# K by DMA transpose, its four taps as diagonal products on TensorE, a full complex product, and one planned order for all engines

## The chip, the cores and the metric

The kernel runs on one core of one Trainium2 chip. A core has a matrix engine (TensorE, PE in the profile, with PEld for its weight loads), a vector engine (VectorE, DVE), an activation engine (ScalarE, ACT), GpSimd (POOL) and SyncE (SP), which here issues every DMA. All share an on-chip memory of 128 partitions; TensorE writes to PSUM, from which VectorE or ScalarE must copy.

The metric is the device time of one execution in microseconds. The kernel before took 290.25 us (median of three runs, 289.12 to 290.41).

## The reference

x is A_q, 2048 rows (time) by 640 columns. Two branches are computed from it and mixed by a gate.

```python
def _A_ref(q, k, v, shift_k, ssm_k, ssm_D):
    k_shift = sum over t of k_pad[:, t:t + S, :] * shift_k[:, ks - 1 - t]     # four taps along time
    kv = k_shift * v
    y = irfft(rfft(kv, 2 * S) * rfft(ssm_k, 2 * S))[:S]                        # a causal convolution, per column
    y = y + kv * ssm_D
    return q * y

def _B_ref(x, w1, w2, w3, w4):
    h = gelu(layernorm(x) @ w1)
    hs = (four groups of h's columns, moved by +1, -1, +2, -2 rows) @ w2
    x1 = x + hs
    return x1 + gelu(layernorm(x1) @ w3) @ w4

g = sigmoid((x * gate_w).sum(-1, keepdims=True))
return g * _A_ref(x, ...) + (1 - g) * _B_ref(x, ...)
```

(The first two lines are shortened: the reference pads, transforms over the padded length 4096 and cuts.) All inputs and the output are bf16; w1 and w2 are 640x640, w3 640x1536, w4 1536x640.

## The kernel before

Time is split as t = 16 p + t1: partition p holds 16 rows, and a "row group" t1 is one row of each partition, 128x640. Branch B works on 128x512 and 128x128 matmuls: `mlp1` (w1, in 4 chunks of 4 row groups, ScalarE applies gelu), `w2` (16 row groups, VectorE adds x and sums), `w3` (4 chunks of 6 pairs) and `w4` (16 row groups). x and x1 are normalized by `x_stats`, `x_transpose` and `x1_norm` and transposed by DMA from SBUF.

Branch A's transform of length 4096 is done as four passes of small matmuls, with a trip through DRAM between them. `step1` multiplies the 64 time points of each row group with the table F1, for the filter h (8 calls on HT) and for kv (8 calls on KV), and writes to S_h and S_x. `gather` reads these in another order. `step2` multiplies with T2 (32 frequency groups for h and 32 for x, four to a call); the result holds real parts in partitions 0 to 63 and imaginary parts in 64 to 127. `product` multiplies h and x. `step3` multiplies with the inverse tables and writes to S_g, `gin` reads S_g, and `step4` multiplies with F4, with q and the gate, and adds to x1.

In F1 the two halves of the partitions hold even and odd 16-row blocks, so that step1 is two matmuls of 64 rows each, in two halves of the array.

The parts that the change touches:

- **Taps.** `kv_load` brings K in with three rows of halo (18 DMAs on SP), `kv_consts` spreads the tap factors over the partitions, and `kv_compute` works on VectorE alone: per pair of row groups four products with the factors (line 458), three sums (463), one product with v (464).
- **Product.** `product` (lines 365 to 367) makes the two cross products (64 partitions each) and the straight products, three VectorE operations per call. It leaves the real and imaginary sums to step3, which multiplies the straight products with I1 and the cross products with I2 into one PSUM tile (378, 380).
- **Tables.** `table` (289) spreads the sines in CMP to T2, I1 and I2 on GpSimd. They lie in the buffer (tag RT) that HT leaves free after step1.
- **Order.** The string ORDER names the steps. For SP the first 139 names are issued in exactly this order; all other instructions are placed by the framework's scheduler, on each engine, when the program is built. A letter in a step's name says which engine copies from PSUM (A is ScalarE, V VectorE, G GpSimd).

PSUM holds two tiles for branch A (`psc`) and two for branch B (`psm`).

## Time and profile before

| | before |
|---|---|
| median of three runs | 290.25 us |
| the profiled execution | 289.77 us, its span 288.0 us |
| busy: TensorE, VectorE, ScalarE, GpSimd | 237.0, 233.1, 161.8, 67.2 us |
| mean granted TensorE clock | 0.957 |
| DMA | 58.77 MB, mean 204 GB/s |
| VectorE on the taps (lines 458, 463, 464) | 59.9 us |
| table loads of ScalarE | ten, 1283 ns each |

Busy time of TensorE is the union of its matmuls, each from start to modelled end; matmuls overlap, so a busy TensorE is not one at its peak, and its work is better read from start to start. The groups of instructions give, behind the shape and the count, the busy time of the group, the mean of one in ns, and the idle time of the engine just before, with what ended it.

### The profile page before, as it was taken

How to read it: one execution, taken by the hardware profiler on the slowest of the kernel's cores; microseconds unless marked ns; L12 is line 12 of the kernel's file. 1: busy time of each engine (PE TensorE's matmuls, PEld its weight loads, DVE VectorE, ACT ScalarE, POOL GpSimd, SP SyncE). 2: the span in 40 equal slices, each digit the busy share in tenths (PEclk: the TensorE clock that was granted, in tenths of full speed). 3: DMA queues.
4: the chain of work that ended last, by engine and by line, in shares of the span. 5: the costliest groups of instructions: out<-in, count | busy, mean ns of one | idle time of the engine just before them, and what ended most of it. 6: DMA issues, size and time to landing. Idle time of an engine off the chain costs nothing.

```text
span 288.0 us, 4142 instructions
## 1 busy us (share of the span) xinstructions
PE 237.0 (82%) x1486; PEld 114.6 (40%) x1486; DVE 233.1 (81%) x438; ACT 161.8 (56%) x234; POOL 67.2 (23%) x57
## 2 busy tenths in 40 slices
PE   0167499599999799996199999999999999998670
PEld 0023134367554232433034555544455544454330
DVE  3888999979999999779851888689899969622894
ACT  4949896486848699563055425365234566600651
POOL 3122223002878030059871000000010000000442
PEclk9999889879999999999579999999999999999997
DMA  7496894471999589592369964483786660298283
GB/s 263 156 216 124 184 238 93 169 229 36 342 235 260 175 278 378 220 347 107 63 223 321 230 222 138 162 287 98 246 285 210 201 218 23 109 278 333 97 257 114
DMA packets 51692, 58.77 MB, mean 204 GB/s; under 512 B 25427, under 2 KB 42580, under 8 KB 51160
## 3 DMA queue, kind: packets, MB, share of 16 engines
q1 hardware_dynamic: 51672, 58.52, 66.2%
q8 instruction: 11, 0.18, 0.3%
q14 instruction: 9, 0.07, 0.1%
HBM read 34.91 MB, written 18.36 MB: 185 GB/s over the span
## 4 chain that ended last, share of the span: by engine, by line
DVE 45%; PE 29%; DMA 9%; issue 6%; POOL 3%; SPq 3%; ACT 2%; POOLq 0%; DVEq 0%; ACTq 0%
PE ps L639 8%; PE ps L658 6%; DVE tmp L458 5%; DMA q<-in_A_q_dram 4%; PE psw L595 4%; PE ps L354 4%; DVE p L366 4%; DVE hs L367 4%; DVE acc L463 3%; DVE p L365 3%; PE pst L313 2%; PE ps L378 2%; DMA WA<-in_B_w_dram 2%; PE ps L329 2%; DVE xn L471 2%
## 5 line engine op out<-in xcount | busy, mean ns | idle before, releaser
L639 PE MATMUL ps<-x1t,W 128*128 128x512 bf16 x240 | 63.2, 386 | 0.0
L658 PE MATMUL ps<-W,gt 128*128 128x512 bf16 (+1 forms) x384 | 60.7, 300 | 0.0
L331 ACT CAST stg<-ps 128x1024 bf16<-128x1024 f32 (+1 forms) x37 | 31.5, 900 | 22.8 <-PE ps L329 16.9
L658 PEld LDWEIGHTS <-gt 128*128 128x128 bf16 x384 | 28.7, 98 | 23.4 <-issue 2.6
L669 POOL TENSOR_SCALAR q<-q,GS 128x640 bf16<-128x640 bf16 x8 | 8.9, 1121 | 121.6 <-DMA q<-in_A_q_dram 63.3
L530 PE MATMUL psm<-xt,WA 128*128 128x512 bf16 x100 | 25.8, 422 | 10.2 <-DMA xt<-xn 8.6
L640 ACT ACTIVATE gt<-ps 128x1024 bf16<-128x1024 f32 x24 | 24.7, 1033 | 13.0 <-PE ps L639 12.9
L639 PEld LDWEIGHTS <-W 128*128 128x128 bf16 x240 | 21.1, 98 | 24.3 <-issue 3.4
L354 PE MATMUL ps<-ax,TB 128*128 128x512 bf16 (+1 forms) x128 | 26.9, 298 | 0.9 <-DVE gs L384 0.4
L659 DVE SCALAR_TENSOR_TENSOR X<-ps,OMG,X 128x640 bf16<-128x640 f32 x16 | 14.1, 880 | 14.8 <-PE ps L658 14.8
L463 DVE TENSOR_TENSOR acc<-acc,tmp 128x1280 bf16<-128x1280 bf16 x24 | 22.9, 955 | 0.4
L595 PE MATMUL psw<-WA,HT 128*128 128x512 bf16 (+1 forms) x116 | 22.8, 312 | 0.6 <-DVE X L599 0.6
L483 POOL TENSOR_TENSOR rs<-ve,EXPO 128x4 f32<-128x4 f32 x8 | 10.6, 1330 | 53.8 <-DVE ve L613 25.1
L458 DVE TENSOR_TENSOR tmp<-K,cj 128x1280 bf16<-128x1280 bf16 (+1 forms) x25 | 22.9, 921 | 0.2
L530 PEld LDWEIGHTS <-WA 128*128 128x128 bf16 x100 | 10.5, 106 | 29.3 <-issue 20.3
L680 ACT CAST y<-ps 128x640 bf16<-128x640 f32 x15 | 10.1, 693 | 20.0 <-PE ps L676 14.9
L358 DVE CAST hs<-ps 128x640 bf16<-128x640 f32 x15 | 11.9, 817 | 9.8 <-PE ps L354 9.8
L356 ACT CAST hs<-ps 128x640 bf16<-128x640 f32 x17 | 11.7, 694 | 14.0 <-PE ps L354 14.0
L289 POOL TENSOR_SCALAR TB<-CMP,sm 128x2048 bf16<-128x2048 bf16 (+1 forms) x8 | 14.6, 1840 | 19.4 <-ACT stg L331 19.4
L356 ACT CAST xs<-ps 128x640 bf16<-128x640 f32 x15 | 10.2, 692 | 14.4 <-PE ps L354 11.9
L354 PEld LDWEIGHTS <-TB 128*128 128x128 bf16 x128 | 12.1, 97 | 15.2 <-issue 5.3
L382 ACT CAST gs<-ps 128x640 bf16<-128x640 f32 x17 | 11.3, 694 | 12.1 <-PE ps L380 11.8
(130 smaller groups left out, 413.5 us busy)
## 6 DMA issues: line engine op xcount, KB each, us to landing
S_h<-stg SPq DMA_DIRECT2D x8, 640.0 KB, 4.2
...
```

The source lines that it names most:

```text
L289: G.tensor_scalar(out=dst, in0=src, scalar1=col(c), scalar2=0.0, op0=ALU.mult, op1=ALU.add)
L331: A.copy(out=stg[:, :, o:o + w], in_=ps[:, :, 0:w])
L354: PE.matmul(ps[:, o:o + w], lhsT=st["T2"][:, g, :], rhs=ax[:, i, o:o + w], start=True, stop=True)
L356: A.copy(out=dst[:, i, :], in_=ps[:])
L458: V.tensor_tensor(out=dst[:, i:i + n, :], in0=K[:, r:r + n, :], in1=cj[:, j:j + 1, :].to_broadcast([P, n, D]), op=ALU.mult)
L463: V.tensor_tensor(out=acc[:], in0=acc[:], in1=tmp[:], op=ALU.add)
L530: PE.matmul(ps[:, v, :].rearrange("p (a b) -> p a b", a=4), lhsT=W1N[:, k, 160 * f:160 * f + P] if f < 4 else W1M[:, k, :], rhs=xt[:, :, k ...
L595: PE.matmul(ps[:, o:o + w], lhsT=h_tile(f, t1), rhs=W2P[:, f, o:o + w], start=(f == 0), stop=(f == 4))
L639: PE.matmul(ps[:, u, :].rearrange("p (a b) -> p a b", a=4), lhsT=st["W3"][:, k, f * P:(f + 1) * P], rhs=xt[:, :, k, :], start=(k == 0), st ...
L640: A.activation(out=gt[:, 2 * (fp % 2):2 * (fp % 2) + 2, :], in_=ps[:], func=ACT.Gelu_apprx_tanh)
L658: PE.matmul(ps[:, o:o + w], lhsT=st["gt", c, f // 4][:, f % 4, i * P:(i + 1) * P], rhs=st["W4"][:, f, o:o + w], start=(f == 0), stop=(f == ...
L659: V.scalar_tensor_tensor(out=X1[:, t1, :], in0=ps[:], scalar=OMG[:, t1:t1 + 1], in1=X1[:, t1, :], op0=ALU.mult, op1=ALU.add)
```

## The change

- **K.** `k_load` transposes K by DMA, straight from DRAM, in four pieces of four row groups, so that columns lie on partitions and KT holds, per row group and block of 128 columns, a 128x128 matrix. `k_wrap` makes the three row groups that reach back over a partition's edge.
- **Taps.** `kv_consts` builds 20 diagonal matrices (5 column blocks by 4 taps) on VectorE. `tap` (16 row groups) makes, per column block, four matmuls of 128x128x128 with KT as weights and a diagonal matrix as moving operand, added in PSUM: transposing back and weighing at once. Then VectorE multiplies with v, from PSUM (V) or behind a copy by ScalarE (A).
- **Rows.** v, the filter and KV now all use t = 16 p + t1. `h_transpose` makes whole 128x128 transposes in place of two halves. F1 is kept twice, with the partitions of one parity set to zero, and step1's two matmuls use all 128 rows.
- **Product.** Two more VectorE operations of 64 partitions form real and imaginary part; step3 has one table I and one matmul pair per group.
- **Tables.** T2 and I are spread by VectorE (letters VV), four operations of 2048 elements.
- **Scaling.** `scale_x1` and `gate_q` may also use ScalarE.
- **End.** `gin` reads in three pieces (8, 6 and 2 row groups) in place of two, and the stores are steps of their own.
- **Order.** Each step is a generator that yields between its instructions on different engines, and a name in ORDER advances its step by one piece. All five engines are issued in exactly the order of the string; the scheduler places nothing. The string is new.

The diff, cut to its core:

```diff
-    k_flat = A_k.rearrange("b s d -> (b s) d")
+    v_rows = A_v.rearrange("b (p t1) d -> (b p) t1 d", t1=NT)
+    k_rows = A_k.rearrange("b (p t1) d -> (b p) (t1 d)", t1=NT)
...
+    def scaled(ev, dst, src, a):
+        if ev == "A":
+            A.activation(out=dst, in_=src, func=ACT.Copy, scale=a)
+        else:
+            (G if ev == "G" else V).tensor_scalar(out=dst, in0=src, scalar1=a, scalar2=0.0, op0=ALU.mult, op1=ALU.add)
...
+    def piped(pairs):
+        last = None
+        for first, second in pairs:
+            first()
+            yield
+            if last is not None:
+                last()
+                yield
+            last = second
+        last()
...
     def step1(name, c, ev):
-                PE.matmul(ps[:, r, 0:w], lhsT=F1[H * r:H * r + H, :], rhs=src[H * r:H * r + H, 2 * c * D + o:2 * c * D + o + w], start=True, stop=True)
+                    PE.matmul(ps[:, r, 0:w], lhsT=F1[:, r, :], rhs=src[:, 2 * c * D + o:2 * c * D + o + w], start=True, stop=True)
...
     def product(s):
         V.tensor_tensor(out=p2[64:128], in0=x[64:128], in1=h[0:64], op=ALU.mult)
+        yield
         V.tensor_tensor(out=h[:], in0=x[:], in1=h[:], op=ALU.mult)
-        st["p", s] = (h, p2)
+        yield
+        V.tensor_tensor(out=h[0:64], in0=h[0:64], in1=h[64:128], op=ALU.subtract)
+        yield
+        V.tensor_tensor(out=h[64:128], in0=p2[0:64], in1=p2[64:128], op=ALU.add)
+        st["p", s] = h
...
     def step3(s, ev):
-                PE.matmul(ps[:, o:o + w], lhsT=st["I1"][:, g, :], rhs=p1[:, i, o:o + w], start=True, stop=False)
-            for (o, w) in pieces(D):
-                PE.matmul(ps[:, o:o + w], lhsT=st["I2"][:, g, :], rhs=p2[:, i, o:o + w], start=False, stop=True)
+                    PE.matmul(ps[:, o:o + w], lhsT=st["I"][:, g, :], rhs=p1[:, i, o:o + w], start=True, stop=True)
...
+    GIN = ((0, 8), (8, 6), (14, 2))
...
-    def kv_compute(c):
...
+    def kv_consts():
+        st["DG"] = pool("A2").tile([P, DC * 4, P], BF16, name="DG")
+        V.tensor_tensor(out=st["DG"][:], in0=IDB[:].unsqueeze(1).to_broadcast([P, DC * 4, P]),
+                        in1=st["cr"][:].rearrange("p k j -> p (k j)").unsqueeze(2).to_broadcast([P, DC * 4, P]), op=ALU.mult)
+
+    def k_load(c):
+        SP.dma_start_transpose(out=st["KT"][:, 4 * c:4 * c + 4].rearrange("p a b c -> p (a b) c"), in_=k_rows[:, 4 * c * D:4 * c * D + 4 * D])
+
+    def k_wrap(ev):
+        st["KW"] = pool("A2").tile([P, 3, DC, P], BF16, name="KW")
+        turn(G if ev == "G" else V, st["KW"][:].rearrange("p a b c -> p (a b) c"), st["KT"][:, NT - 3:NT].rearrange("p a b c -> p (a b) c"), 1)
+
+    def v_load(c):
+        SP.dma_start(out=st["KV"][:, 4 * c * D:4 * c * D + 4 * D].rearrange("p (t d) -> p t d", d=D), in_=v_rows[:, 4 * c:4 * c + 4, :])
+
+    def tap(t1, ev):
+        ps = psc.tile([P, D], F32, name="psk", tag="c")
+        for k in range(DC):
+            for j in range(4):
+                u = t1 - j
+                PE.matmul(ps[:, k * P:k * P + P], lhsT=st["KT"][:, u, k, :] if u >= 0 else st["KW"][:, u + 3, k, :], rhs=st["DG"][:, 4 * k + j, :],
+                          start=(j == 0), stop=(j == 3))
+        yield
+        kv = st["KV"][:, t1 * D:t1 * D + D]
+        if ev == "A":
+            y = ring.tile([P, D], BF16, name="yk", tag="gq", bufs=3)
+            A.copy(out=y[:], in_=ps[:])
+            yield
+            V.tensor_tensor(out=kv, in0=y[:], in1=kv, op=ALU.mult)
+        else:
+            V.tensor_tensor(out=kv, in0=ps[:], in1=kv, op=ALU.mult)
...
+        "open.L1.left open.A2.right kv_alloc consts0 load_cj load_x.2 consts0 k_load.1 t2_table kv_consts "
+        "x_stats.2.AAAA x_stats.2.AAAA k_load.2 t2_table x_stats.2.AAAA x_stats.2.AAAA x_stats.2.AAAA f1_table t2_table "
...
     def emit(names):
         for n in names:
-            f, *args = n.split(".")
-            calls[f](*(int(a) if a.isdigit() else a for a in args))
+            if n not in steps:
+                f, *args = n.split(".")
+                steps[n] = calls[f](*(int(a) if a.isdigit() else a for a in args))
+            if steps[n] is not None:
+                next(steps[n], None)
-    with tc.manual_schedule(engines={mybir.EngineType.SP}):
-        emit(ORDER[:FIRST])
-    emit(ORDER[FIRST:])
+    with tc.manual_schedule(engines={getattr(mybir.EngineType, n) for n in ("PE", "DVE", "Activation", "Pool", "SP")}):
+        emit(ORDER)
```

Three places show what the order now is. The first is SP's queue at the start of the program (X is x, WA holds w1, cr the tap factors, KV first holds v). Before:

```order
L153 DMA X<-in_A_q_dram 128x2560
L156 DMA WA<-in_B_w_dram 128x5x640
L401 DMA cr<-in_A_shift_k_dram 1x2560
L153 DMA X<-in_A_q_dram 128x2560 x2
L479 DMA_TRANSPOSE xt<-xn 128x20x128
L153 DMA X<-in_A_q_dram 128x2560
L479 DMA_TRANSPOSE xt<-xn 128x20x128
L479 DMA_TRANSPOSE xt_268<-xn 128x20x128 x2
```

Now:

```order
L464 DMA cr<-in_A_shift_k_dram 128x5x4
L153 DMA X<-in_A_q_dram 128x2560
L478 DMA_TRANSPOSE KT<-in_A_k_dram 128x20x128 x2
L486 DMA KV<-in_A_v_dram 128x2560 x2
L478 DMA_TRANSPOSE KT<-in_A_k_dram 128x20x128 x2
L486 DMA KV<-in_A_v_dram 128x2560 x2
L153 DMA X<-in_A_q_dram 128x2560
L156 DMA WA<-in_B_w_dram 128x5x640
L370 DMA S_x<-stg 256x1x1280
L153 DMA X<-in_A_q_dram 128x2560
```

K and v come first, behind one chunk of x; w1 and the rest of x come behind them, and the third chunk of x behind step1's first write.

The second place is VectorE at a product (p and hs are products, ps a PSUM tile, X<-ps the sum of w4). Before:

```order
L365 TENSOR_TENSOR p_1853<-xs,hs 64x2560
L358 CAST hs<-ps_1839 128x640
L366 TENSOR_TENSOR p_1853<-xs,hs 64x2560
L659 SCALAR_TENSOR_TENSOR X<-ps_1857,OMG,X 128x640
L367 TENSOR_TENSOR hs<-xs,hs 128x2560
```

Now:

```order
L411 TENSOR_TENSOR p_2033<-xs,hs 64x2560
L413 TENSOR_TENSOR p_2033<-xs,hs 64x2560
L415 TENSOR_TENSOR hs<-xs,hs 128x2560
L717 SCALAR_TENSOR_TENSOR X<-ps_2025,OMG,X 128x640
L417 TENSOR_TENSOR hs<-hs 64x2560
L419 TENSOR_TENSOR hs<-p_2033 64x2560
```

There are five operations in place of three between the copies.

The third place is TensorE in step3, one frequency group. Before:

```order
L378 LDWEIGHTS TB
L378 MATMUL ps_1775<-hs,TB 128x512
L378 LDWEIGHTS TB
L378 MATMUL ps_1775<-hs,TB 128x128
L380 LDWEIGHTS TB
L380 MATMUL ps_1775<-p_1635,TB 128x512
L380 LDWEIGHTS TB
L380 MATMUL ps_1775<-p_1635,TB 128x128
```

Now, with w4 (L714) behind a pair of groups:

```order
L431 LDWEIGHTS TB
L431 MATMUL ps_2035<-hs,TB 128x512
L431 LDWEIGHTS TB
L431 MATMUL ps_2035<-hs,TB 128x128
L431 LDWEIGHTS TB
L431 MATMUL ps_2040<-hs,TB 128x512
L431 LDWEIGHTS TB
L431 MATMUL ps_2040<-hs,TB 128x128
L714 LDWEIGHTS gt
L714 MATMUL ps_2025<-W_1474,gt 128x512
```

Each group has half the matmuls.

More of the change, by code (lines that the diff above doesn't have):

```diff
@@ L278, in i_tables @@
             n = tab([P, NG, 32], "n")
[L279 to L292 removed]
+            ts(n[:], m[:], col(20 + c), op0=ALU.add)
@@ new lines, in i_tables, with table @@
+            yield from sin_table(CMP[:, 1, :, c, :], n, 8192)
+            yield
[4 more added lines that the diff above has]
+            (G if ev == "G" else V).tensor_scalar(out=dst, in0=src, scalar1=a, scalar2=0.0, op0=ALU.mult, op1=ALU.add)
+    def table(which, ev):
+        if "I" not in st:
+            TB = main.tile([P, 2, NG, P], BF16, name="TB", tag="RT")
+            st["T2"], st["I"] = TB[:, 0], TB[:, 1]
@@ L304, in h_transpose, with pair, first, second @@
     def h_transpose(dc):
-        if dc == 0:
+        if "HT0" not in st:
             st["HT0"] = main.tile([P, NT * D], BF16, name="HT0", tag="RT")
-        hv = st.pop(("HN", dc)).rearrange("p (t2 r t1) -> p t1 r t2", t1=NT, r=2)
+        hv = st.pop(("HN", dc)).rearrange("p (t t1) -> p t1 t", t1=NT)
         dst = st["HT0"][:].rearrange("p (t d) -> p t d", t=NT)
-        for hh in range(2):
+        def pair(hh):
             ps = psc.tile([P, 8, P], BF16, name="pst", tag="c")
-            for i in range(8):
-                for r in range(2):
-                    PE.transpose(out=ps[H * r:H * r + H, i, :], in_=hv[:, 8 * hh + i, r], identity=IDB[:])
-            f = A.copy
-            f(out=dst[:, 8 * hh:8 * hh + 8, dc * P:(dc + 1) * P], in_=ps[:])
+            def first():
+                for i in range(8):
+                    PE.transpose(out=ps[:, i, :], in_=hv[:, 8 * hh + i, :], identity=IDB[:])
+            def second():
+                A.copy(out=dst[:, 8 * hh:8 * hh + 8, dc * P:(dc + 1) * P], in_=ps[:])
+            return first, second
@@ L317, in d_fold @@
+        yield from piped(pair(hh) for hh in range(2))
     def d_fold():
@@ L345, in step2, with pair, first, second @@
         ax = st.pop((name, s))
[L346 to L350 removed]
+        dst = []
+        def pair(i):
             g = 4 * s + i
             ps = psc.tile([P, D], F32, name="ps2", tag="c")
[L353 to L359 removed]
+            def first():
+                for (o, w) in pieces(D):
+                    PE.matmul(ps[:, o:o + w], lhsT=st["T2"][:, g, :], rhs=ax[:, i, o:o + w], start=True, stop=True)
+            def second():
+                if not dst:
+                    if name == "h":
+                        dst.append(pool("L2").tile([P, 4, D], BF16, name="hs", tag="hp", bufs=4))
+                    else:
+                        dst.append(pool("C").tile([P, 4, D], BF16, name="xs", tag="xs", bufs=2))
+                    st[name + "s", s] = dst[0]
+                if ev[i] == "A":
+                    A.copy(out=dst[0][:, i, :], in_=ps[:])
+                else:
+                    V.tensor_copy(out=dst[0][:, i, :], in_=ps[:])
+            return first, second
+        yield from piped(pair(i) for i in range(4))
     def product(s):
@@ L388, in gin @@
+        yield from piped(pair(i) for i in range(4))
+        for u in range(2):
+            yield
+            g = 4 * s + 2 * u
+            SP.dma_start(out=bass.AP(tensor=S_g[:].tensor, offset=S_g[:].offset + g * P * D, ap=[[D, P], [P * D, 2], [1, D]]), in_=st["gs", s, u][:])
+    GIN = ((0, 8), (8, 6), (14, 2))
     def gin(q, a):
+        t, n = GIN[q]
         if ("gin", q) not in st:
-            st["gin", q] = (R1("gin0") if q == 0 else pool("L3").tile([P, NT * D], BF16, name="gin1"))[:].rearrange("p (r d) -> p r d", r=2)
@@ L403, in kv_consts @@
[L403 to L417 removed]
+        st["cr"] = ring.tile([P, DC, 4], BF16, name="cr", tag="cr", bufs=1)
```

269 lines of the change are left out of this document (119 added, 150 removed), and 125 rows, old and new, of the table ORDER.

## The prediction

> **What bounds the kernel now.** I read the page first (busy shares and the chain that ended last), then busy time by stretch, then the chain in order of time.
>
> ```profile
> span 288.0 us, 4142 instructions
> PE 237.0 (82%) x1486; PEld 114.6 (40%) x1486; DVE 233.1 (81%) x438; ACT 161.8 (56%) x234; POOL 67.2 (23%) x57
> DVE 45%; PE 29%; DMA 9%; issue 6%; POOL 3%; SPq 3%; ACT 2%; POOLq 0%; DVEq 0%; ACTq 0%
> ```
>
> VectorE and TensorE are equally busy, and the chain runs over VectorE first, over TensorE second. The stretches show that this is not one limit but three, one after another:
>
> ```profile
> 0.00:17.00 17.00, 1.86 (x4) 0.59 (x5) 10.81 (x64) 11.70 (x27) 4.53 (x11) 1.00 0.71 209
> 17.00:36.00 19.00, 13.60 (x49) 5.39 (x49) 17.48 (x65) 15.11 (x21) 4.45 (x4) 0.96 0.78 171
> 36.00:140.00 104.00, 91.58 (x644) 44.05 (x643) 96.31 (x176) 71.72 (x102) 40.44 (x29) 0.94 0.70 215
> 140.00:160.00 20.00, 17.00 (x78) 6.86 (x78) 9.53 (x16) 9.83 (x11) 8.95 (x6) 0.82 0.78 232
> 160.00:252.00 92.00, 90.33 (x559) 45.61 (x558) 78.32 (x84) 42.94 (x59) 0.79 (x1) 1.00 0.58 187
> 252.00:288.00 36.00, 22.63 (x156) 12.12 (x153) 20.70 (x37) 10.52 (x16) 8.08 (x7) 0.94 0.63 216
> ```
>
> The columns are span, then busy time of TensorE, its weight loads, VectorE, ScalarE, GpSimd, then granted clock, DMA share and GB/s. Until 140 us VectorE is the limit (96.31 of 104 in the third stretch). TensorE is busy there too by the record, but it waits between short matmuls. From 160 to 252 TensorE is full (90.33 of 92). The last 36 us belong to waits:
>
> ```profile
> 127.66 2.37 DVE tmp L458
> ...
> 252.46 4.91 DMA S_g<-gs
> ...
> 259.07 7.73 DMA q<-in_A_q_dram
> ...
> 272.73 4.69 DMA q<-in_A_q_dram
> ...
> 284.58 0.49 DVE X L684
> ```
>
> In the tail the chain goes through the last write of S_g and two loads of q. The first row is of another kind: a tap product of 2.37 us, in the stretch in which GpSimd builds the tables.
>
> **The change, part by part.** VectorE first, with the rows that carry its prices:
>
> ```profile
> L458 DVE TENSOR_TENSOR tmp<-K,cj 128x1280 bf16<-128x1280 bf16 (+1 forms) x25 | 22.9, 921 | 0.2
> L463 DVE TENSOR_TENSOR acc<-acc,tmp 128x1280 bf16<-128x1280 bf16 x24 | 22.9, 955 | 0.4
> L458 DVE TENSOR_TENSOR acc<-K,cj 128x1280 bf16<-128x1280 bf16 (+1 forms) x9 | 7.5, 844 | 0.0
> L464 DVE TENSOR_TENSOR KV<-acc,KV 128x1280 bf16<-128x1280 bf16 x8 | 6.6, 827 | 0.1
> L367 DVE TENSOR_TENSOR hs<-xs,hs 128x2560 bf16<-128x2560 bf16 x8 | 11.9, 1489 | 0.2
> L365 DVE TENSOR_TENSOR p<-xs,hs 64x2560 bf16<-64x2560 bf16 x8 | 11.9, 1487 | 0.9 <-ACT hs L356 0.5
> L366 DVE TENSOR_TENSOR p<-xs,hs 64x2560 bf16<-64x2560 bf16 x8 | 11.9, 1484 | 0.1
> L358 DVE CAST xs<-ps 128x640 bf16<-128x640 f32 x17 | 13.7, 821 | 5.3 <-PE ps L354 5.1
> L681 DVE TENSOR_TENSOR y<-y,q 128x640 bf16<-128x640 bf16 x15 | 8.0, 551 | 0.7 <-POOL q L669 0.7
> L669 DVE TENSOR_SCALAR q<-q,GS 128x640 bf16<-128x640 bf16 x8 | 2.9, 382 | 2.1 <-DMA q<-in_A_q_dram 2.1
> L659 DVE SCALAR_TENSOR_TENSOR X<-ps,OMG,X 128x640 bf16<-128x640 f32 x16 | 14.1, 880 | 14.8 <-PE ps L658 14.8
> ```
>
> *Taps leave VectorE:* 22.9 + 22.9 + 7.5 + 6.6 = 59.9 us, all before 142 us, where VectorE sets the pace. *What comes for them:* of the 16 row groups ten go through ScalarE and one multiply (10 x 551 ns = 5.5), six are multiplied from PSUM (6 x 0.82 = 4.9). The 20 diagonal matrices are one product of 2560 elements: between L367's 1.49, whose operands lie side by side, and 2.9 (twice that, since one operand is a repeated element); I take 2.7. *The full product:* two more 64-partition operations per group, 8 x 2 x 1.49 = +23.8. *Copies:* by the order 23 of step2's 64 stay with VectorE (32 before) and 5 of step3's 32 (15 before): 19 x 0.82 = -15.6. *Tables:* the four operations of 2048 elements come from GpSimd: 0.38 (L669, 640 elements) to 1.22 (3.2 times that); I take 1.0, +4. They wait for step1's last read of HT, whose buffer the tables take; TensorE has w4's first groups beside them. Net about -35.
>
> ScalarE takes the copies, and loses table loads (ten before; the order has three):
>
> ```profile
> L331 ACT CAST stg<-ps 128x1024 bf16<-128x1024 f32 x26 | 25.7, 1026 | 21.6 <-PE ps L329 15.7 <-issue 4.6 <-DMA S_x<-stg 0.7
> L601 ACT ACTIVATE jk<-X 128x640 bf16<-128x640 bf16 x16 | 11.9, 743 | 5.2 <-DVE X L599 4.3 <-DVE ve L613 0.9
> L356 ACT CAST xs<-ps 128x640 bf16<-128x640 f32 x15 | 10.2, 692 | 14.4 <-PE ps L354 11.9 <-issue 2.5
> L208 ACT ACT_TABLE_LOAD x4 | 5.1, 1283 | 0.1
> ```
>
> (19 + 10 - 3) x 0.69 = +18, eleven scalings near L601's 0.74 = +8, seven loads less = -9. That is work beside other work, as long as ScalarE is not the longest engine of its stage.
>
> TensorE, by rows that give start to start:
>
> ```profile
> 60.25 1.99 PE L313 MATMUL pst<-IDB,E 128*64 128x128 bf16 x32
> ...
> 85.87 0.22 PE L595 MATMUL psw<-WA,HM 128*128 128x128 bf16 x1
> 86.05 4.48 PE L639 MATMUL ps<-x1t,W 128*128 128x512 bf16 x20
> 90.45 0.61 PE L329 MATMUL ps<-HT,F 64*128 64x512 bf16 x4
> 90.99 1.04 PE L595 MATMUL psw<-WA,HT 128*128 128x512 bf16 x4
> ...
> 208.68 0.61 PE L658 MATMUL ps<-W,gt 128*128 128x128 bf16 x8
> ```
>
> Twenty 512-wide matmuls take 4.48, and the next row starts 4.40 behind them: 220 ns each with the change of form at the end, and I use 216. One 128-wide matmul is on record for 0.22 from start to end, eight of them, each with its own weights, for 0.61: (0.61 - 0.22)/7 = 56 ns from start to start. *Taps:* 16 x 20 x 56 = +17.9. *step3:* one matrix in place of two, 32 x (216 + 56) = -8.7. *step1:* L329's two pairs, side by side, take 0.54 (90.45 to 90.99); with zeros in half the rows the four go one after another, 0.86; over 16 groups, the 256-wide piece included, about +6 (0 to 8.7). *h_transpose:* 160 halves at 62 ns become 80 whole ones at 56 to 125: 0 to -5.5, I take -4. Net +11, in the stages where TensorE idled.
>
> *DMA:* four transposes replace 18 issues of K:
>
> ```profile
> L479 SPq DMA_TRANSPOSE xt<-xn x4: 3019/3069/3158, 12.1 to 27.4; - x4
> ```
> ```profile
> xt<-xn SPq DMA_TRANSPOSE x4, 5.0
> ```
> ```profile
> 3.00:9.00 6.00, 1.86 (x4) 0.49 (x4) 4.00 (x30) 4.05 (x9) 0.11 (x1) 1.00 1.03 402
> 20.00:22.00 2.00, 2.00 (x9) 0.86 (x8) 1.72 (x7) 2.00 (x7) 0.27 (x1) 1.00 1.12 216
> ```
>
> The three rows are x's transposes by issue (least, median, most ns), their landing, and two stretches, the first with plain loads alone, the second with a transpose alone. A transpose of K's size holds SP's queue 3.07 us, lands 5.0 us after issue and moves 216 GB/s where plain loads move 402. These read SBUF; K's will read DRAM, which no row shows: from 3.07 us up, and I take 3.07. Then the two that the first taps need land near 10 us, and all four near 17; VectorE and ScalarE have the tables and a chunk's statistics until then. Behind them on SP stand v, X's chunk 0 and w1. Behind step1's first write to S_x, which waits for its last copy, stand X's chunks 1 and 3: a late chunk of KV delays the statistics too.
>
> **The sum, by stage of the new order.** I counted each engine's instructions between places in the order and priced them by these rows. (1) Up to mlp1's first matmul: TensorE 21, ScalarE 38 (18 passes of statistics, ten copies of taps, six of step1, sines, two table loads), VectorE 37 (the 10.81 + 17.48 of the first 36 us of before hold the same tables and statistics; less 8.7 for the copies of cj and for statistics and normalization that now come later, plus 17 for the taps, their matrices, three copies and F4's table). Before, ScalarE stood idle 9.2 of its first 36 us; with that, 47. (2) mlp1 until w2 starts: TensorE 29.2 (100 x 216 and the rest of step1 and taps), the others 16 to 24. (3) w2 and the filter's step1: TensorE 48.2, ScalarE 47.9. (4) step2 to step3: TensorE 96.3; VectorE 59.6 for products, 22 for copies, 10.6 (12 x 0.88) for w4 and 6 for shorter ones, 98 (the tables' 4 stand beside stage 3's end). (5) step4 and the last of w4: TensorE 28.2, and 4 for the last sum and store; q's last load stands on SP behind two stores that wait for step4's first sums, with some 15 us of TensorE's work ahead of its use. Stages 2 to 5 run at the share that the busiest engine reaches: 96.31/104 = 0.93 or 90.33/92 = 0.98; I take 0.955. So 47 + 30.6 + 50.5 + 102.7 + 29.5 + 4 = 264.3 us of span. Span to time is 289.77 - 288.0 = 1.8: **266 us** (the profiled run lies 0.5 below the median of 290.25, which is less than the rounding here). Against before: stages 1 to 3 end at 128, where TensorE's full stretch begins at 160 now (-32), stage 4 takes 103 where that stretch took 92 (+11), and the tail is 33.5 where it was 36 (-2.5).
>
> **Rivals.**
>
> *A. The order works nearly without waits.* Stages 2 to 5 at 0.98, stage 1 at 44 us: 44 + 29.8 + 49.2 + 100 + 28.8 + 4 = 256, time 258. For it: 160:252 shows 0.98 already, and GpSimd, beside which a tap took 2.37 us, loses the tables. Against: stage 3 has two engines within 1%, stage 4 two within 2%; in 160:252 VectorE had only 78 of 92.
>
> *B. VectorE bounds stage 4.* Each group now waits for 7.4 us of products (4.5 before) between step2 and step3. If neither engine hides the other and the busier reaches 0.85: 98/0.85 = 115, 12.6 more, 279 us. Against: w3 and w4, 70 us of TensorE's 96, do not depend on the products.
>
> *C. Slower: K's transposes from DRAM.* All of stage 1 hangs on them: no tap, no KV, and behind them on SP no X and no w1. At 216 GB/s they run at half of the 402 of plain loads. If their small pieces go at a third of that out of DRAM, each holds the path 9 us instead of 3, stage 1 grows by 4 x 6 = 24 and the time is 290; it is slower than before from about 9.5 us each. The Trainium skill ("DMA: Bandwidth & Descriptors", Specifications) puts line rate at transfers of 512 B and up, which speaks for this; how far below it DRAM lies, no row shows.
>
> *D. A cold TensorE in stage 1.*
>
> ```profile
> PEclk9999889879999999999579999999999999999997
> ```
>
> Each digit is a fortieth of the span, 7.2 us. The 5 stands at 137 to 144 us, right behind a stretch without matmuls: there TensorE had half its clock. In stage 1 it has 21 us of work in 47. At half clock the 320 taps cost 112 ns each, 36 us instead of 18, and with step1's the stage 42 us of TensorE beside 38 and 37 of the others. Three equal engines at 0.85 make 49, with six of the ten us ahead of the first tap 55: 8 more, 274 us. Against it: the first 36 us of before show 0.96 to 1.00 with TensorE idle for more than half. The Trainium skill ("TensorE: Matmul & The Clock Gate", Part 1) says that an idle window of about 3.4 us halves the clock until a busy one passes; the row agrees, and by that rule D would hold wherever taps wait that long for a chunk.
>
> *E. No change:* B, stage 3 at 0.85 as well (48.2/0.85 = 56.7, +6), and a tail like the old one (+2.5) make 288.
>
> **How the numbers follow.** Forecast 266 (257 to 276) 0.45; A 0.20; B 0.13; D 0.10; E 0.03; C 0.09. Differences under 0.5% of 290 (1.5 us) can't be told from none. The forecast, A, B and D are faster; of their 0.88 I move one hundredth to no change: faster 0.87, same 0.04, slower 0.09. The range goes from 250, which leaves out the part of A in which stage 1 hides as well (0.06), to 286, which leaves out C, E and some of B (0.13).
>
> **What would show it.** Right: 16 groups of taps of 20 matmuls at 56 to 107 ns start to start, no VectorE row of 1280 elements; each K transpose on SP near 3 us; mlp1's first matmul near 47 us; step2's first near 128; the last store within 5 us of the last matmul; VectorE's products at 1.5 us each, 40 of them. Wrong: K's landing beyond 8 us each (C), a stage from step2 to step3 over 110 us with TensorE waiting for hs (B), an mlp1 that starts after 55 us with a clock near 0.5.

## The result and the profile after

| | before | after |
|---|---|---|
| median | 289.69 us (4 runs, 289.0 to 290.41) | 273.39 us (4 runs, 272.99 to 275.34) |
| ratio | | 0.945, 95% interval 0.940 to 0.951 |
| span and mean granted clock of the profiled execution | 288.0 us, 0.957 | 271.9 us, 0.969 |

The change saves 16.3 us. The forecast was 266 us, in a range from 250 to 286. The direction and the way are as forecast; the time is 7.4 us above it, and all of that lies in one stage.

The page of the changed kernel, its busy time, its clock and its chain of waits:

```profile
PE 237.8 (87%) x1635; PEld 133.5 (49%) x1657; DVE 198.8 (73%) x376; ACT 174.4 (64%) x261; POOL 43.6 (16%) x54
PEclk9995999999999999999999999997799979999999
PE 53%; issue 21%; DVE 13%; ACT 7%; POOL 2%; DMA 2%; another core or an unknown queue 1%; ACTq 0%; SPq 0%; DVEq 0%; POOLq 0%
```

VectorE went from 233.1 to 198.8 us (-34.3; the prediction has about -35), and the chain that ended last now runs over TensorE first (53%, before 29%), with VectorE at 13% instead of 45%. Of the 21% "issue" nearly all is one piece of 51 us in which GpSimd waits, by which the chain was traced past the filter's work, so the chain is not read further there. The clock has three low places, one at 20 to 27 us and two from 187 us on.

The prediction's five stages, in the view of busy time by stretch (columns as before: span, then TensorE, its weight loads, VectorE, ScalarE, GpSimd, clock, DMA share, GB/s):

```profile
0.00:47.00 47.00, 27.31 (x321) 23.04 (x326) 38.19 (x131) 33.64 (x62) 5.23 (x13) 0.93 0.87 253
47.00:76.00 29.00, 28.89 (x180) 14.47 (x180) 15.91 (x44) 20.95 (x26) 9.68 (x21) 1.00 0.95 257
76.00:127.00 51.00, 50.68 (x347) 28.52 (x352) 27.56 (x70) 44.62 (x70) 18.93 (x13) 1.00 0.82 250
127.00:240.00 113.00, 103.18 (x610) 52.56 (x616) 97.78 (x95) 61.51 (x87) 8.18 (x6) 0.95 0.53 162
240.00:272.00 32.00, 27.71 (x186) 14.93 (x187) 19.39 (x40) 13.72 (x19) 1.60 (x2) 1.00 0.70 246
```

By the first and last matmuls of each step the borders are:

| stage | predicted | measured |
|---|---|---|
| 1, up to mlp1's first matmul | 47 | 46.5 |
| 2, until w2 starts | 30.6 | 29.5 |
| 3, until step2 starts | 50.5 | 51.3 (step2 at 127.3) |
| 4, until step3 ends | 102.7 | 112.2 (at 239.4) |
| 5, to the end | 33.5 | 32.5 |

Stage 4 is 9.5 us longer than predicted, the other four together 1.8 us shorter. So the experiments ask mainly about stage 4, in which neither VectorE (97.8 of 113 us) nor TensorE (103.2, a part of it at half clock) is full.

The groups that answer to the prices:

```profile
L493 PE MATMUL psk<-DG,KT 128*128 128x128 bf16 x290 | 22.5, 241 | 13.9 <-DMA KT<-in_A_k_dram 11.6
L501 DVE TENSOR_TENSOR KV<-yk,KV 128x640 bf16<-128x640 bf16 x10 | 4.6, 485 | 1.1 <-ACT yk L499 1.1
L473 DVE TENSOR_TENSOR DG<-IDB,cr 128x2560 bf16<-128x2560 bf16 x1 | 2.8, 2816 | 0.0
L419 DVE TENSOR_TENSOR hs<-p 64x2560 bf16<-64x2560 bf16 x8 | 11.9, 1490 | 0.2
L478 SPq DMA_TRANSPOSE KT<-in_A_k_dram x4: 3255/3840/5342, 1.8 to 16.1; - x4
```

The diagonal matrices took 2.8 us (2.7 taken), an operation of the full product 1.49 (1.49), a multiply of the taps 0.485 (0.551). K's transposes hold SP's queue 3.3 to 5.3 us each, median 3.84, where x's row had given 3.07.

### The profile page after: what moved, and what is told of

It reads as the page before. It is cut to its first block, busy times and chain, and to the rows that moved or that the text cites. A ratio compares the mean times of both kernels' runs of the same rounds, so it can differ in the third digit from the quotient of the medians.

```text
span 271.9 us, 4369 instructions
## 1 busy us (share of the span) xinstructions
PE 237.8 (87%) x1635; PEld 133.5 (49%) x1657; DVE 198.8 (73%) x376; ACT 174.4 (64%) x261; POOL 43.6 (16%) x54
## 4 chain that ended last, share of the span: by engine, by line
PE 53%; issue 21%; DVE 13%; ACT 7%; POOL 2%; DMA 2%; another core or an unknown queue 1%; ACTq 0%; SPq 0%; DVEq 0%; POOLq 0%
PE ps L696 14%; PE psm L573 8%; PE psw L650 8%; PE ps L714 8%; PE ps L357 5%; PE psk L493 2%; PE ps L431 2%; PE pst L333 2%; PE ps L390 2%; DMA X<-in_A_q_dram 2%; ACT jk L537 2%; PE ps L734 1%; DVE X L745 1%; DVE X L717 1%; DVE b L543 1%
## 5 line engine op out<-in xcount | busy, mean ns | idle before, releaser
L714 PE MATMUL ps<-W,gt 128*128 128x128 bf16 (+1 forms) x376 | 59.1, 300 | 0.6 <-issue 0.2
L696 PE MATMUL ps<-x1t,W 128*128 128x512 bf16 x240 | 55.7, 380 | 0.1
L714 PEld LDWEIGHTS <-gt 128*128 128x128 bf16 x384 | 29.4, 99 | 21.1 <-issue 1.5
L493 PE MATMUL psk<-DG,KT 128*128 128x128 bf16 x290 | 22.5, 241 | 13.9 <-DMA KT<-in_A_k_dram 11.6
L493 PEld LDWEIGHTS <-KT 128*128 128x128 bf16 x290 | 20.7, 110 | 14.7 <-DMA KT<-in_A_k_dram 11.6
L365 DVE CAST stg<-ps 128x512 bf16<-128x512 f32 (+1 forms) x17 | 14.3, 845 | 13.3 <-PE ps L357 11.8
L652 DVE SCALAR_TENSOR_TENSOR X<-psw,X 128x640 bf16<-128x640 f32 x16 | 13.2, 823 | 11.8 <-PE psw L650 10.4
L650 PE MATMUL psw<-WA,HT 128*128 128x128 bf16 (+1 forms) x112 | 21.3, 296 | 0.3
L431 PE MATMUL ps<-hs,TB 128*128 128x512 bf16 x64 | 14.1, 317 | 4.1 <-ACT gs L438 1.6
L295 POOL TENSOR_SCALAR X<-X,OMG 128x640 bf16<-128x640 bf16 x7 | 6.8, 980 | 63.2 <-DVE xn L673 51.2
L357 PE MATMUL ps<-KV,F 128*128 128x512 bf16 (+1 forms) x42 | 11.8, 361 | 5.8 <-DVE KV L503 2.5
```

The source lines that it names most:

```text
L357: PE.matmul(ps[:, r, 0:w], lhsT=F1[:, r, :], rhs=src[:, 2 * c * D + o:2 * c * D + o + w], start=True, stop=True)
L431: PE.matmul(ps[:, o:o + w], lhsT=st["I"][:, g, :], rhs=p1[:, i, o:o + w], start=True, stop=True)
L493: PE.matmul(ps[:, k * P:k * P + P], lhsT=st["KT"][:, u, k, :] if u >= 0 else st["KW"][:, u + 3, k, :], rhs=st["DG"][:, 4 * k + j, :], star ...
L650: PE.matmul(ps[:, o:o + w], lhsT=h_tile(f, t1), rhs=W2P[:, f, o:o + w], start=(f == 0), stop=(f == 4))
L696: PE.matmul(ps[:, u, :].rearrange("p (a b) -> p a b", a=4), lhsT=st["W3"][:, k, f * P:(f + 1) * P], rhs=xt[:, :, k, :], start=(k == 0), st ...
L714: PE.matmul(ps[:, o:o + w], lhsT=st["gt", c, f // 4][:, f % 4, i * P:(i + 1) * P], rhs=st["W4"][:, f, o:o + w], start=(f == 0), stop=(f == ...
```

## Experiments

"Stage 4" is always the time from step2's first matmul to step3's last, 112.2 us in the changed kernel.

### The written order for SyncE alone

```diff
-    with tc.manual_schedule(engines={... "PE", "DVE", "Activation", "Pool", "SP"}):
+    with tc.manual_schedule(engines={mybir.EngineType.SP}):
```

> The changed kernel with one part undone: the written order binds SyncE alone, as it did before, and for the other engines it is only the order in which steps are handed to the scheduler. Nothing is left out of the computation; the rows of TensorE move at a handful of places, mostly the filler w4 around the filter's products. If the hand-written order of all engines carries part of the gain (the rival of 258 us rested on it): slower by 3 to 10 us, 277 to 283. If the gain is the work taken off VectorE and the order only records what a scheduler would do too: within 2 us of the changed kernel's 273.4. My own view: the second, 0.6.

Measured: 282.84 us, ratio to before 0.978 (0.972 to 0.984). My view was wrong: undoing the order of the four other engines costs 9.4 us of the 16.3. It isn't lost in one place. mlp1 starts 2.1 us later (48.6), step2 4.7 later (132.0), stage 4 is as long (112.1), and from step3's end to step4's first matmul it takes 13.3 us instead of 9.1. The SP queue shows the last of these. First the changed kernel, then this one: the last writes of S_g, the first reads, and step4's first matmul (a row with x2 or x3 joins neighbouring issues, from the start of the first to the end of the last).

```profile
238.97 1.87 SPq L447 DMA_DIRECT2D S_g<-gs  x2
242.06 1.45 SPq L459 DMA_DIRECT2D gin<-S_g  x2
...
248.56 1.25 PE L734 MATMUL ps<-gin,F 128*128 128x512 bf16 x8
```
```profile
237.94 7.50 SPq L447 DMA_DIRECT2D S_g<-gs  x3
245.92 2.04 SPq L459 DMA_DIRECT2D gin<-S_g  x2
...
257.35 1.25 PE L734 MATMUL ps<-gin,F 128*128 128x512 bf16 x8
```

### The feed-forward's filler spread over stage 4

From 172 to 193 us the changed kernel has no matmuls of w3 or w4 between the filter's, from 193 us on it has many. Here chunk 3 changes places with chunk 2, and the steps of both are spread; the last stores follow in another order (an excerpt of ORDER):

```diff
- step3.1 step3.1 product.5 step3.1 step3.1 step3.1 step3.1 product.5 ... step2.x.6 step2.x.6 ...
+ step3.1 step3.1 product.5 step3.1 w3.3.0 step3.1 step3.1 step3.1 product.5 ... step2.x.6 w3.3.1 w3.3.0 step2.x.6 ...
```

> The changed kernel with the feed-forward's filler moved in stage 4 and nothing else: the chunk whose transposed rows are there since 165 us (w3 and w4 of chunk 3) comes ahead of chunk 2, and its matmuls are spread evenly over 172 to 239 us, where the changed kernel has none in 172 to 193 and everything from 193 on. Nothing is left out. Theory A (the 9.5 us that stage 4 is over its predicted 102.7 are the stretch without filler, in which TensorE is busy 2.4 to 4.1 of 5 us and its clock then falls to 0.62): these 7 to 8 us of TensorE's idle time come back, 264 to 268 us. Theory B (VectorE bounds stage 4: 96.9 of 112 us busy, and its products wait for the evacuations whatever TensorE does in between): at most 2 us, 271 to 274. Theory C (the filler in the stretch delays the evacuations that ScalarE has to do, 5.00 of 5 us busy there, since its gelu comes on top): slower, 275 to 280. A 0.5, B 0.35, C 0.15.

Measured: 287.35 us, ratio 0.993 (0.990 to 0.996), so 14 us slower than the changed kernel. Stage 4 takes 123.5. It went further the wrong way than the third theory had it, and the stretches show how:

```profile
180.00:190.00 10.00, 8.27 (x44) 3.88 (x42) 4.33 (x5) 7.43 (x12) 6.19 (x4) 1.00 0.56 200
190.00:200.00 10.00, 8.15 (x43) 3.85 (x43) 5.32 (x6) 7.55 (x11) 0.00 (x0) 1.00 0.91 198
200.00:210.00 10.00, 6.68 (x44) 3.57 (x44) 9.80 (x10) 3.47 (x6) 0.00 (x0) 0.94 0.81 282
210.00:220.00 10.00, 6.25 (x35) 2.94 (x33) 9.83 (x11) 1.38 (x2) 0.00 (x0) 0.84 0.11 46
```

Until 200 us the filter's matmuls wait behind filler (ten matmuls of w3 take 2.32 us in one piece) and its copies behind gelu (1.04 us each), and VectorE stands at half (4.33 and 5.32 of 10); once it waits 5.48 us for a matmul of step2. Product 6 starts at 195.8 instead of 188.9 us. Then VectorE is full (9.80, 9.83) and the filler that would have run beside it is used up: TensorE 6.25, ScalarE 1.38. In the changed kernel matmuls of w3 and w4 stand beside the full VectorE:

```profile
195.00:200.00 5.00, 5.00 (x27) 2.40 (x26) 4.88 (x6) 3.07 (x4) 0.00 (x0) 1.00 0.81 282
```

So missing filler was the wrong reading of 172 to 193 us. In this kernel filler pays where VectorE sets the pace, and costs where matmuls and copies take turns; how much of the cost is the filler's matmuls and how much its gelu, this run doesn't separate.

### Two of the product's five operations left out

```diff
         V.tensor_tensor(out=h[:], in0=x[:], in1=h[:], op=ALU.mult)
-        yield
-        V.tensor_tensor(out=h[0:64], in0=h[0:64], in1=h[64:128], op=ALU.subtract)
-        yield
-        V.tensor_tensor(out=h[64:128], in0=p2[0:64], in1=p2[64:128], op=ALU.add)
```

> The changed kernel without the last two operations of each full product, the subtraction and the sum (16 instructions of 1.49 us on VectorE, 23.8 us); the filter's part of the output is then not the product. All else stays, step3 with its one matmul pair too. If VectorE bounds stage 4 (theory B, and my rival of 279 us): 16 to 24 us faster, 249 to 257. If TensorE with the filler bounds it (102 of 112 us busy, my forecast's stage 4): 6 to 12 us faster, 261 to 267, since no more of TensorE's time than its 10 us idle can be had. If the chain through the evacuations of ScalarE and PSUM bounds: under 5 us.

Measured: 272.31 us (269.97 to 272.74), ratio 0.940 (0.934 to 0.947). With 23.8 us less for VectorE the time is 1.1 us lower, which this run can't tell from none; stage 4 takes 110.2. VectorE's work does not bound stage 4 in this order. What is left is the stretch in the middle, as long as before though VectorE has room:

```profile
170.00:180.00 10.00, 7.64 (x48) 3.91 (x47) 7.00 (x8) 9.20 (x15) 1.55 (x2) 1.00 0.58 180
180.00:190.00 10.00, 6.42 (x32) 2.83 (x30) 5.84 (x6) 8.03 (x14) 3.47 (x3) 1.00 1.06 299
190.00:200.00 10.00, 8.39 (x34) 3.58 (x34) 6.31 (x7) 4.21 (x7) 0.00 (x0) 0.83 0.90 279
```

### Six copies from ScalarE to VectorE, with five and with three operations

ScalarE is the fullest engine there (9.20, 8.03), so I moved copies to VectorE:

```diff
- step3.1.AAAA   step2.x.6.AAAA   step3.4.AAAA
+ step3.1.AVAV   step2.x.6.AVAV   step3.4.AVAV
```

> The changed kernel with three groups' copies out of PSUM between 170 and 183 us shared: two of the four copies each of step3.1, of step2.x.6 and of step3.4 go to VectorE in place of ScalarE (six copies, 6 x 0.63 = 3.8 us off ScalarE, 6 x 0.82 = 4.9 us onto VectorE), in the same places of the order. Nothing is left out. Theory D (the stretch from 172 to 193 us without filler is bound by copies: TensorE waits after each pair of 0.43 us for a copy of 0.63, ScalarE 5.00 of 5 us): the stretch becomes 2 to 4 us shorter, 269 to 271.5. Theory B (VectorE, 4.9 of 5 us there too, with product 5): product 5 and with it step3.5 come 4.9 us later, 275 to 279. If both are full, neither: 272 to 275. 0.4, 0.35, 0.25.

> Both edits together: the last two operations of each product left out (the filter's part is then not the product; 23.8 us off VectorE, which alone gave 272.3) and the six copies between 170 and 183 us moved to VectorE, which now has room for them (7.0 and 5.8 of 10 us busy). Theory D (copies bound the stretch): 4 to 6 us faster than without the copies' move, 266 to 268. If the stretch waits for something else (rows out of DRAM, the transposition behind GpSimd): within 1.5 us of 272.3.

Measured: 278.79 us, ratio 0.963 (0.960 to 0.965), and with three operations 275.78, ratio 0.952 (0.949 to 0.954): 5.4 and 3.5 us slower than the same kernels without the move, both against the theory that the number of copies sets the pace. The second can't be VectorE's load, since that kernel has room. The timeline of it (start, duration, engine, line; in brackets the idle time before, and what ended it):

```profile
175.44 0.43 PE L427 MATMUL ps<-hs,TB 128*128 128x512 bf16 x2 [0.82 <-ACT gs L434]
175.83 1.49 DVE L413 TENSOR_TENSOR p<-xs,hs 64x2560 bf16<-64x2560 bf16 x1
...
176.36 0.69 ACT L400 CAST xs<-ps 128x640 bf16<-128x640 f32 x1 [0.97 <-PE ps L390]
177.11 0.43 PE L390 MATMUL ps<-ax,TB 128*128 128x512 bf16 x2 [0.82 <-ACT xs L400]
177.35 0.82 DVE L436 CAST gs<-ps 128x640 bf16<-128x640 f32 x1
178.20 1.49 DVE L415 TENSOR_TENSOR hs<-xs,hs 128x2560 bf16<-128x2560 bf16 x1
178.22 0.69 PE L390 MATMUL ps<-ax,TB 128*128 128x512 bf16 x2 [0.68 <-DVE gs L436]
178.95 0.69 ACT L400 CAST xs<-ps 128x640 bf16<-128x640 f32 x1 [1.89 <-PE ps L390]
```

VectorE does its instructions in the order written. The copy of 0.82 us starts at 177.35, where the product of 1.49 that began before it ends, and branch A has two PSUM tiles: one is held by that copy, the other passes through ScalarE, which then waits for TensorE (0.97, 1.89), which waits for VectorE (0.68). From 178 us on two matmuls take 0.69 where they took 0.43: with TensorE at 2.27 of 5 us the clock has fallen, and it stays at half until 195 (two of the rows):

```profile
175.00:180.00 5.00, 2.27 (x9) 0.93 (x9) 4.91 (x6) 1.78 (x3) 0.00 (x0) 0.76 0.65 236
180.00:185.00 5.00, 4.18 (x14) 1.56 (x13) 3.73 (x6) 2.08 (x3) 3.28 (x2) 0.50 0.71 229
```

So this stretch hangs on the time until a copy is done, its wait in the engine's queue included, and not on an engine's sum. How much of the 5.4 and 3.5 us is that wait and how much the half clock behind it, no run separates.

### Four steps of GpSimd to VectorE

```diff
- x1_norm.2.VVVG   scale_x1.8.G   scale_x1.9.G   scale_x1.10.G
+ x1_norm.2.VVVV   scale_x1.8.V   scale_x1.9.V   scale_x1.10.V
```

> The changed kernel with the five steps that GpSimd does between 181 and 188 us (a quarter of chunk 2's normalization, scalings of three rows) done by VectorE, in the same places of the order. Nothing is left out. The trace of the changed kernel has ScalarE waiting 1.85 us behind GpSimd there, with two evacuations behind it, TensorE 1.87 us, and the transposition that w3 of chunk 2 needs starts at 185.9. If that hold is what costs: 2 to 4 us faster, 269.5 to 271.5 (VectorE takes 1.6 us more of its own). If it lies beside a bound elsewhere (VectorE full, theory B): no change or 1 us slower, 273 to 275. 0.6 for the first.

It is four steps, not five: one quarter of the normalization and three scalings. Measured: 272.60 us (271.81 to 272.91), ratio 0.942 (0.937 to 0.948); stage 4 110.7, so 1.5 shorter. By the time alone it can't be told from the changed kernel. TensorE still waits 1.61 us in one piece for a copy of VectorE, and the clock still falls, to 0.50 and 0.53 from 185 to 195 us. Two more holds of this kind stood in the trace of the changed kernel, and the next run takes all three.

### Three holds of one engine behind another

The first two holds in the changed kernel:

```profile
182.68 1.72 DVE L673 TENSOR_SCALAR xn<-X,m,rs 128x640 bf16<-128x640 bf16 x2
183.31 2.56 POOL L673 TENSOR_SCALAR xn<-X,m,rs 128x640 bf16<-128x640 bf16 x1
...
184.32 0.81 DVE L402 CAST xs<-ps 128x640 bf16<-128x640 f32 x1
185.19 0.70 PE L390 MATMUL ps<-ax,TB 128*128 128x512 bf16 x4 [1.87 <-DVE xs L402]
...
185.90 0.83 ACT L293 ACTIVATE X<-X,OMG 128x640 bf16<-128x640 bf16 x1 [1.85 <-POOL xn L673]
```

The first is ScalarE's scaling of a row, which waits 1.85 us until GpSimd has read it and has two copies behind it. The second is the copy at 184.32, for which TensorE waits 1.87 us: it stands on VectorE behind two passes of the normalization (182.68, 1.72 us), not behind a product, which had ended at 182.65. The third is two copies of step2.h.2 between VectorE's products at 214 to 218 us, where TensorE waits 1.20 us. The edit is the one above, and

```diff
- step2.x.7.AAAV   step2.h.2.VAVA
+ step2.x.7.AAAA   step2.h.2.AAAA
```

> The changed kernel without three holds of one engine behind another that its trace shows: GpSimd's five steps at 181 to 188 us go to VectorE (alone 272.6), the last copy of step2.x.7 (TensorE waits 1.87 us for it behind VectorE's product) and two copies of step2.h.2 (1.20 us, ScalarE idle 3.70 us before) go to ScalarE. Nothing is left out. If each of these waits is on the path: 269 to 271. If the time goes into the next wait, the transposition of x1t.2 or the S_g write: 272 to 273.5. 0.55, 0.45.

Measured: 270.28 us (6 runs, 269.07 to 271.02), ratio 0.932 (0.928 to 0.936). Stage 4 takes 107.2, 5.0 us less, with the same work. From the start of stage 4, 2.4 of these are there at step2.h.2's first matmul (behind the first two holds), 2.0 more at step2.x.2's (behind the third, where the clock stays up too), and 0.5 come later. The clock stays up:

```profile
180.00:185.00 5.00, 3.56 (x18) 1.54 (x17) 4.50 (x9) 4.90 (x9) 0.00 (x0) 1.00 0.87 309
185.00:190.00 5.00, 2.90 (x16) 1.33 (x15) 4.30 (x6) 3.72 (x6) 0.00 (x0) 1.00 1.15 310
```

In the changed kernel these were, with the row behind them, and the two rows at the third hold:

```profile
180.00:185.00 5.00, 2.40 (x12) 1.05 (x11) 4.49 (x6) 3.53 (x6) 3.77 (x2) 1.00 0.93 340
185.00:190.00 5.00, 3.46 (x14) 1.52 (x14) 2.84 (x4) 3.00 (x5) 2.41 (x3) 0.70 1.09 242
190.00:195.00 5.00, 4.58 (x18) 1.79 (x17) 4.90 (x5) 3.15 (x5) 0.00 (x0) 0.62 1.03 295
...
215.00:220.00 5.00, 3.25 (x27) 1.95 (x26) 4.91 (x5) 2.22 (x4) 0.42 (x1) 1.00 0.60 189
220.00:225.00 5.00, 4.58 (x16) 1.97 (x17) 4.90 (x6) 3.93 (x7) 0.79 (x1) 0.66 0.39 136
```

### Extra matmuls against the fall of the clock

```diff
+    def warm(n):
+            PE.matmul(ps[:, 0:n], lhsT=st["W3"][:, 0, 0:P], rhs=st["W3"][:, 1, 0:n], start=True, stop=True)
- step2.x.7 step2.x.7 x1_norm.2 step2.x.7 step2.x.7 x1_norm.2 ...
+ step2.x.7 warm.512 step2.x.7 x1_norm.2 step2.x.7 warm.512 step2.x.7 x1_norm.2 ...
```

The tile `ps` is one of psm's, and nothing reads it.

> The changed kernel with 21 extra matmuls between 172 and 193 us (12 of 256 columns, 9 of 512) on rows of w3, whose result nothing reads: some 12 x 0.11 + 9 x 0.22 = 3.3 us of TensorE in a stretch in which it is idle for 6.5 of 20 us, with no copy behind them. Nothing is left out. They ask nothing of ScalarE and VectorE, which the filler of the earlier run did. Theory E (part of stage 4's excess is the granted clock that falls to 0.70 and 0.62 behind this idle stretch, 185 to 194 us): the digits there stay at 1, and 2 to 3.5 us come back, 270 to 271.5. If the fall costs nothing, since the copies set the pace: 273 to 275; if the extra matmuls only stand in the way: 275 to 277. 0.4, 0.35, 0.25.

> Both: the three holds removed and the 21 extra matmuls. Nothing is left out. By theory E and by the holds together 267 to 269.5; without theory E, the same as with the holds alone, 0 to 3 us more.

Measured: 271.55 us (6 runs, 271.13 to 271.77), ratio 0.937 (0.933 to 0.941), and together with the three holds removed 269.25, ratio 0.930 (0.925 to 0.934). In the first the clock is 1.00 from 170 to 195 us and from 210 to 225, and stage 4 takes 109.8, 2.4 us less, though the 1.87 us wait is still there. Only 0.7 of these are there at step2.h.2's first matmul, behind the place of the extra matmuls. Another 1.1 come between there and step2.x.2's first, around 220 us, where the edit adds nothing and TensorE has the same waits (1.20, 0.55 and 0.16 us), but the clock doesn't fall this time; why it doesn't, no run shows. The rest comes later. In the second stage 4 takes 107.3, no less than without the extra matmuls; its first matmul of mlp1 came 1.4 us earlier, in a stage that the edit doesn't touch, but in which the clock was back sooner (0.98 from 25 to 30 us, against 0.69 with the holds alone removed). So the two falls of the clock in stage 4 were worth some 2 us together, and whoever removes the waits doesn't need the extra matmuls.

### Stage 1: K by plain transfers, and extra matmuls

```diff
-        SP.dma_start_transpose(out=st["KT"][...], in_=k_rows[...])
+        SP.dma_start(out=st["KT"][...], in_=k_rows[...])
```

> The changed kernel with K's four transposing transfers as plain transfers of the same rows into the same tile (K is then not transposed, so the taps' products are of wrong operands; the filter's part is not the reference's). It prices the transposition and shows what stage 1 hangs on. In the changed kernel they take 3.9 to 4.3 us of SyncE's queue each and land after 6.1, and TensorE waits 11.6 us for the first. If stage 1 (46.5 us) hangs on K's arrival: the first tap 3 to 5 us earlier and mlp1's first matmul 3 to 6 us earlier, 267 to 271. If stage 1 is bound by VectorE's and ScalarE's tables and statistics (about 37 us each in 46.5): mlp1 within 1.5 us of 46.5, 272 to 274. 0.4 and 0.6.

Measured: 273.59 us (272.41 to 274.08), ratio 0.944 (0.941 to 0.947): no difference. TensorE's wait for K falls from 11.6 to 9.1 us, but mlp1 starts at 47.8 instead of 46.5. TensorE is through the first taps earlier and then waits 3.8 us in one piece for ScalarE's copy of a tap, and its clock is at half from about 15 to 29 us, longer than with the transposition (0.55, 0.50 and 0.58 in the stretches from 15 to 30, against 0.97, 0.50 and 0.85). So the transposition isn't what stage 1 hangs on, and the clock is a part of it. The last run tests that, on the version without the three holds: 90 extra 128-wide matmuls before the first tap, 40 before step1's first.

```diff
+            PE.matmul(ps[:, 0:P], lhsT=IDB[:], rhs=IDB[:], start=True, stop=True)
- f1_table tap.10.A ...           x_stats.2.AAAA step1.KV.4.AAV ...
+ f1_table warm.90 tap.10.A ...   x_stats.2.AAAA warm.40 step1.KV.4.AAV ...
```

> The version without the three holds (270.3, clock 0.50 from about 20 to 26 us) with 130 extra matmuls on the identity in stage 1, whose result nothing reads: 90 before the first tap, where TensorE waits until 11.1 us for K, and 40 before step1's first, where it waits until 20.3 us for VectorE. Nothing is left out. This is my rival D by itself. If the half clock is on the path of stage 1: the taps behind it (60 of them took 4.97 us, 83 ns each, in the changed kernel, against 56 at full clock) lose some 1.6 us, step1's first copies another 0.5, and mlp1's first matmul moves from 46.9 to 44.5 to 45.5, time 268 to 269.3. If ScalarE and VectorE (about 37 us each in 47) set the stage: within 0.7 us of 270.3, with the clock at 1. If the extra matmuls hold up step1: 271 to 273. 0.4, 0.45, 0.15.

Measured: 267.49 us (6 runs, 266.62 to 269.04), ratio 0.928 (0.924 to 0.931), the fastest of all versions. The median is 2.8 us under the one without extra matmuls, but the kernel before, timed beside each, was 1.0 us faster here too (288.49 against 289.54), and the intervals of the two ratios overlap; 1.3 us is what the ratios give. The trace shows the place: mlp1 starts at 44.5 instead of 46.9, and the profiled execution is 1.8 us shorter. The stretches without and with the extra matmuls:

```profile
20.00:25.00 5.00, 3.63 (x25) 2.72 (x27) 4.37 (x19) 2.97 (x3) 1.07 (x2) 0.63 0.96 341
25.00:30.00 5.00, 4.38 (x46) 4.08 (x45) 1.34 (x5) 2.19 (x5) 0.00 (x0) 0.69 1.01 354
```
```profile
20.00:25.00 5.00, 3.63 (x47) 2.64 (x45) 4.58 (x20) 3.67 (x4) 1.12 (x2) 1.00 1.00 310
25.00:30.00 5.00, 3.74 (x49) 2.75 (x46) 3.15 (x7) 3.98 (x8) 0.00 (x0) 1.00 1.01 348
```

In the ten microseconds after 20 TensorE gets through 92 matmuls of the taps and step1 instead of 71 (four of the 96 in the rows are extra ones), and ScalarE through 7.65 us of work instead of 5.16. Some of the clock's fall has only moved forward (0.81 and 0.85 from 10 to 20 us), to where TensorE waits anyway.

### Before, with one tap on VectorE

```diff
-            for j in (2, 1, 0):
-                mul(tmp, j)
-                V.tensor_tensor(out=acc[:], in0=acc[:], in1=tmp[:], op=ALU.add)
```

> The kernel before, with one of K's four taps: three tap products and three sums per pair of row groups are left out (48 instructions, 22.9 + 22.9 us of VectorE), so the filter's input is not the full short convolution. It measures by itself what the taps on VectorE cost before. If VectorE bounds the first 140 us, as the prediction says: most of the 45.8 us, 25 to 40 us off the 289.8, 250 to 265. If the stages behind take it back (TensorE was busy 91.6 of the 104 us from 36 to 140): 8 to 15 us, 275 to 282. If the taps lay beside TensorE's work: under 4 us. 0.35, 0.5, 0.15.

Measured: 281.17 us, ratio 0.969 (0.965 to 0.974). Of 45.8 us of VectorE's work only 8.4 reach the end. step2 starts at 147.3 instead of 156.2 us, and stage 4 takes 95.4 in both. By the busy times TensorE bounds the stretch from 36 us on without these taps:

```profile
36.00:131.00 95.00, 90.64 (x637) 44.48 (x645) 57.29 (x128) 71.67 (x102) 32.91 (x26) 0.98 0.79 235
```

It has 90.64 us of work there, against 91.58 of the same length of program before, in 9 us less.

## Why the prediction came out as it did

**What bounds the kernel now: right in direction, too simple.** VectorE had 96.31 of 104 us in the third stretch, but TensorE with its 91.58 stood right behind it. Without three of the four taps it gave 8.4 us, not 45.8. "VectorE is the limit" was true only down to TensorE's work. The prediction did keep to this in its sum by stages, where each stage has the busier engine's time, and that is why it holds while the single terms would not. The two runs that take one part by itself give 8.4 us (three of the four taps, in the kernel before) and 9.4 us (the order, in the new one), together a little over the 16.3 of the whole change. The other parts (the rows, the tables, the scalings, the end) have no run that undoes them alone.

**Stages 1, 2, 3 and 5: right within 1.1 us each.** The prices from the old trace held: 2.82 us for the diagonal matrices, 1.49 for the two new operations of each product, 97.8 us of VectorE in stage 4 for a predicted 98. Stage 1 came out in part by luck: ScalarE took 33.6 us where the sum has 38, and TensorE 27.3 where it has 21, a part of them at half clock.

**Stage 4: the term that was mis-sized, 102.7 predicted, 112.2 measured.** The step that failed is "stages 2 to 5 run at the share that the busiest engine reaches; I take 0.955". VectorE reached 97.8 of 113, 0.87. The share was read from old stretches in which filler lies between all the filter's matmuls; the new order has a stretch without, from 172 to 193 us, where short matmuls, two PSUM tiles and copies take turns. There no engine's sum bounds the time, and a share of the busiest doesn't apply. Shown by runs: 5.0 of the 9.5 us go when three places are removed in which a copy waits behind another engine's or its own engine's longer instruction; keeping the clock up without removing them brings 2.4, so up to about 2 of the 5.0 can be the clock that falls behind these waits. The remaining 4.5 us are not settled. That the turns between two PSUM tiles cost them is what the timeline suggests; a third tile for branch A was not tried.

**Rival A (order without waits, 258): the order carries half of the result, though not down to 258.** I gave it 0.20 as an addition to the forecast. But the order is worth 9.4 us of the 16.3 by the run that undoes it for four engines, and with the holds and the cold start removed the same work takes 267.5. The prediction has no term for the order; it is hidden in the shares of all stages.

**Rival B (VectorE bounds stage 4, 279): its sign appeared, its cause didn't.** I had named "a stage from step2 to step3 over 110 us with TensorE waiting for hs" as its mark. The stage has 112 us, and TensorE does wait for hs. Taking 23.8 us away from VectorE changed the time by 1.1. The mark was too weak: a wait for hs is a wait for a copy, and tells nothing of the products.

**Rival C (slow transposes of K, 290): the price was in its direction, without effect.** 3.84 us each in the median instead of 3.07, landing after 6.1 instead of 5.0; plain transfers in their place leave the time as it is.

**Rival D (a cold TensorE in stage 1, 274): true in kind, smaller.** The clock is at half from about 20 to 27 us, and in the version without holds extra matmuls that keep it up in that time bring 2.4 us in mlp1's start, where D had 8. Two other traces agree: where the clock was back by 25 us mlp1 started at 45.6, and where it was at half until 29 (K by plain transfers) at 47.8. The stage came out at 46.5 nevertheless; ScalarE's work, priced at 38, took 33.6, which may have made up for it. The Trainium skill ("TensorE: Matmul & The Clock Gate", Part 1) has the clock halved after an idle window of about 3.4 us. The trace agrees that the clock falls behind little work, but no gap from 172 to 187 us was longer than 1.87 us, and it fell all the same, with 2.40 of 5 us busy; with 2.90 of 5 it did not in one version, and with 3.25 of 5 it did at 220 us.

**E (no change)** didn't come. Its terms add up to 287 us (266 + 12.6 + 6 + 2.5), not 288.

**The full product** was priced at +23.8 us of VectorE in stage 4. It was hidden nearly whole: the sum had it in VectorE's 98, which did not set the end.
